# The second stage of two more token blocks by seven products of quarters

## The chip, the cores and the metric

The kernel runs on one core of a Trainium2 chip. Its engines are TensorE (PE), VectorE (DVE), ScalarE (ACT) and GpSimd (POOL); loads and stores are issued mostly by SyncE (SP). The metric is the device time of one execution in microseconds. Before the change three runs took 969.06, 969.94 and 973.84 us (median 969.94).

## The reference

Three layers in a row, on 3072 tokens, in float32:

```
# 1. attention with a decaying state, 4 batches x 8 heads x 768 steps, width 64
state = gamma * state + k_t v_t^T ;  y_t = scale * q_t state
# 2. first stage: x is [3072, 512]
xn  = x / sqrt(mean(x*x) + 1e-6) * rms_g
x2  = (silu(xn @ w_gate) * (xn @ w_val)) @ w_out      # 512 -> 1536 -> 512
# 3. second stage
h   = x2 @ w_in                                       # 512 -> 1024
s   = h * softmax(h)
out = ((s - mean) / sqrt(var + 1e-6) * g_ln) @ w_out2 # 1024 -> 512
```

The weights come as 64-bit numbers and are converted on the chip.

## The kernel before

The tokens are cut into six blocks of 512. A number is kept as a high part in a reduced format and a low part, the remainder (`split`: ACT casts, DVE or POOL subtracts), and each product is three matmuls (`mm3`): high x high, high x low, low x high. Tokens run along the free dimension in the first stage (`bc_block`: twelve tiles of gate and value into the banks GB and VB, each followed by its part of w_out into the four banks X) and along the partitions in the second, in four slices of 128 tokens.

The second stage is written twice. `de_block` takes a slice through eight products with w_in (`d_mm`), the maximum, exponential and mean (`soft`), eight transposes with a new split (`t_tr`), and the last matmul (`e_mm`). `de_quarters` cuts x2 and w_in into quarters and gets the four quarters of h from seven products of sums of quarters instead of eight; the sums of x2 (S1 to S4) are made at its start by DVE and ACT out of the X banks, the sums of w_in (T1, T2, T3 in the scratch tensors `t2scr`, T4 in place) once, by `w2_sums`. T2 and T3 lie in the tiles xnh and xnl, which between second stages hold the normalised tokens. Blocks 4 and 5 also do gate and value by seven products (`SEVEN`), for which `sums_steps` makes sums of the gate and value tiles (the table `SUMS` says in which block).

Block 0's second stage can't follow its first one, since w_in is converted only in block 1 (`w2_fin`). So its X banks are stored (`x2_store`), and `de_block` runs for block 0 behind block 1's. `FIRST7 = 2` is the first block whose second stage uses quarters.

The attention of block n+1 runs beside block n: `att_pieces` gives scores (`att_scores`) and output (`att_out`) of four chunks, which are put at numbered slots. In blocks 2 to 4 they lie in the first stage; in block 1 they begin at slot 35, the second stage. The same slots hold the norm's steps (`rms_steps`), weight loads and sums. What is emitted there gets its place on the engines from a scheduler; each engine then runs its instructions strictly in that order. In the order listings L122 is an attention matmul, and a name such as `X_68` is the bank X0.

Of the kernel before, what the change touches and what calls it, by code (L numbers as in the profile page):

```python
# [9 lines left out]
F32 = mybir.dt.float32  # L10
# [9 lines left out]
NB = 6  # L20
# [16 lines left out]
SUMS = {1: [(3, 0), (3, 1)], 2: [(0, 0), (1, 0), (4, 0)], 3: [(0, 1), (1, 1), (2, 0), (2, 1), (4, 1)]}  # L37
LATE_SUMS = {(3, 2): (5, 0), (3, 24): (5, 1)}
W2_SUMS_AT = (12, 18)
FIRST7 = 2  # L40
# [3 lines left out]
def retention_moe_kernel(ctx: ExitStack, tc: tile.TileContext, qk0, q2, kt, kv, wpk, w2i, w2o,  # L44
# [564 lines left out]
    def sums_steps(j, part, n):  # L609

        X, H = [], []
        tags = {(1, 0): ("A", "r2"), (3, 1): ("x2", "r2")}.get((n, part) if n == 1 or j < 2 else None, ("x2", "x2"))

        def pair(t):
            tag = tags[t is H]
            if tag == "x2":
                x = wt("x2", [P, 2, 512], F32, 4)
                t.extend((x[:, 0, :], x[:, 1, :], x))
            else:
                t.extend(wt(tag, [P, 512], F32, {"A": 2, "r2": 8}[tag]) for _ in range(2))  # L620
# [49 lines left out]
    def w2_sums(k):  # L670
# [3 lines left out]
        def whole():  # L674
            for r in (k, k + 2):
                W.append(wt("x2", [P, 2, 512], F32, 4))
# [16 lines left out]
        def parts2():  # L693
            for i in range(2):
                o.append(wt("st", [P, 512], F32R, 3))
# [101 lines left out]
    def w2_fin(key):  # L797
# [19 lines left out]
    def w_plan():  # L817
# [11 lines left out]
        w2 = [("in", i) for i in range(8)] + [("out", i) for i in range(8)]  # L829
# [357 lines left out]
    x2h, x2l = {}, {}  # L1187

    def d_mm(n, t, s):
        H = HB[t]  # L1190
        ts_ = slice(t * P, t * P + P)
        order = [(k, hf) for k in range(NK) for hf in range(2)] if t == 0 else \
            [(k, hf) for hf in range(2) for k in range(NK)]
        for i, (k, hf) in enumerate(order):
            cs = slice(hf * 512, hf * 512 + 512)
            mm3(H[hf], x2h[k][:, ts_], x2l[k][:, ts_], w2["h"][:, k, cs], w2["l"][:, k, cs],
                k == 0, k == NK - 1)
            if i == 3:
                slot(n, s)
        soft(n, t, H, halves(f4()), f4(), t == NCB - 1)  # L1200
        slot(n, s + 1)
# [53 lines left out]
    def e_mm(n, t, s, bank=None, final=False, nxt=None):  # L1255
# [29 lines left out]
        later = nxt in range(FIRST7, NB) and nxt not in SEVEN  # L1285
# [5 lines left out]

    def x2_split(srcs):
        for d in range(NK):
            if d % 2 == 0:
                th, tl = wt("x2", [P, 2, 512], F32R, 4), wt("x2", [P, 2, 512], F32R, 4)
            x2h[d], x2l[d] = th[:, d % 2, :], tl[:, d % 2, :]
            split(x2h[d], x2l[d], srcs[d])
# [8 lines left out]

    def x2_load():
# [414 lines left out]
```

## Time and profile before

| | |
|---|---|
| median of three runs | 969.94 us |
| the profiled execution | 974.37 us |
| its span, first to last instruction | 972.5 us |
| PE, DVE, ACT, POOL busy | 98%, 58%, 43%, 48% of the span |
| granted clock of PE, mean | 0.99 |

Times in views are microseconds from the start of the span. Block 1's second stage begins at 264, block 0's ends at 358 to 365, block 2's begins at 480. A busy PE is modelled: matmuls overlap, so their pace is read from starts, not from durations. What an engine waited for is put down to whatever signalled it last.

### The profile page before, as it was taken

The page shows a single profiled execution, that of the slowest core. Times are in us where ns is not written, and L with a number is a line of the kernel's source. Part 1 is how long each engine was busy: PE and PEld are TensorE (multiplying, and loading weights), DVE is VectorE, ACT ScalarE, POOL GpSimd, SP SyncE. Part 2 cuts the span into 40 slices and gives each one's busy share as a digit, 9 for nine tenths or more (in the row PEclk, how much of TensorE's full clock was granted, in tenths as well). Part 3 has the DMA queues.
Part 4 walks back from the last instruction along what each step waited for, and adds up shares of the span by engine and source line. Part 5 has one row for each costly group of instructions (what it writes and reads, how often), then busy time and mean ns, then how long its engine had stood idle before and what let it go on. Part 6 is the DMA issues. An engine that isn't in the chain of part 4 may idle for free.

```text
span 972.5 us, 18176 instructions
## 1 busy us (share of the span) xinstructions
PE 954.6 (98%) x6852; PEld 804.2 (83%) x6852; DVE 564.0 (58%) x1126; ACT 417.8 (43%) x831; POOL 465.9 (48%) x497
## 2 busy tenths in 40 slices
PE   8899999999999999999999999999999999999998
PEld 7777887888887888878888888888999888999986
DVE  4787776476375653476574644575655567343473
ACT  3767655476234352223454232356221356221344
POOL 6886764697044483774538455637111176000022
PEclk8899999999999999999999999999999999999999
DMA  9699999998823305799824899923999936698501
GB/s 341 231 317 403 335 312 359 318 348 256 301 73 99 99 22 170 247 323 290 335 76 120 265 336 305 358 101 120 279 301 380 298 115 219 216 306 292 185 0 44
DMA packets 99207, 230.91 MB, mean 237 GB/s; under 512 B 11696, under 2 KB 38704, under 8 KB 98096
## 3 DMA queue, kind: packets, MB, share of 16 engines
q1 hardware_dynamic: 90336, 204.59, 64.2%
q10 hardware_dynamic: 8784, 25.17, 6.7%
q8 instruction: 54, 0.88, 0.4%
q14 instruction: 33, 0.27, 0.1%
HBM read 187.77 MB, written 41.94 MB: 236 GB/s over the span
## 4 chain that ended last, share of the span: by engine, by line
PE 79%; DVE 6%; DMA 5%; POOL 4%; ACT 3%; issue 1%; SPq 0%; ACTq 0%; POOLq 0%; DVEq 0%
PE X L845 9%; PE X L847 9%; PE X L846 9%; PE VB L963 5%; PE GB L845 5%; PE GB L846 5%; PE GB L847 5%; PE VB L845 4%; PE VB L846 4%; PE VB L847 4%; PE GB L963 4%; PE SB L122 3%; PE X L1377 3%; PE GB L1377 2%; PE VB L1377 2%; PE YB L963 2%
## 5 line engine op out<-in xcount | busy, mean ns | idle before, releaser
L846 PE MATMUL X<-r,wo 128*128 128x512 f32 x252 | 98.9, 392 | 0.0
L847 PE MATMUL X<-r,wo 128*128 128x512 f32 x252 | 98.1, 390 | 0.0
L845 PE MATMUL X<-r,wo 128*128 128x512 f32 x252 | 95.5, 395 | 1.0 <-ACT r L101 1.0
L746 POOL TENSOR_TENSOR st<-st,x 128x512 int32<-128x512 int32 x52 | 70.5, 1356 | 53.8 <-DVE st L745 20.0
L101 ACT CAST r<-f 128x512 fp32r<-128x512 f32 x60 | 37.2, 620 | 90.9 <-DVE f L866 71.1
L866 DVE TENSOR_TENSOR f<-VB,f 128x512 f32<-128x512 f32 x48 | 33.0, 688 | 65.6 <-PE VB L847 50.3
L845 PE MATMUL GB<-xnh,w 128*128 128x512 f32 (+1 forms) x172 | 67.8, 394 | 1.0 <-ACT xnh L404 1.0
L845 PE MATMUL VB<-xnh,w 128*128 128x512 f32 (+1 forms) x172 | 67.6, 393 | 1.1 <-DVE f L866 1.1
L282 POOL TENSOR_TENSOR U<-U,u 128x256 f32<-128x256 f32 x27 | 17.5, 648 | 104.5 <-PE YB L122 50.6
L846 PE MATMUL GB<-xnl,w 128*128 128x512 f32 (+1 forms) x172 | 67.1, 390 | 0.3 <-DVE xnl L102 0.3
L846 PE MATMUL VB<-xnl,w 128*128 128x512 f32 (+1 forms) x172 | 66.9, 389 | 0.0
L847 PE MATMUL VB<-xnh,w 128*128 128x512 f32 (+1 forms) x172 | 66.8, 389 | 0.0
L847 PE MATMUL GB<-xnh,w 128*128 128x512 f32 (+1 forms) x172 | 66.7, 388 | 0.0
L102 DVE TENSOR_TENSOR r<-f,r 128x512 fp32r<-128x512 f32 x60 | 55.7, 930 | 18.9 <-ACT r L101 18.2
L897 ACT ACTIVATE f<-GB 128x512 f32<-128x512 f32 x48 | 28.5, 594 | 79.4 <-PE GB L847 79.3
L102 POOL TENSOR_TENSOR r<-st,r 128x512 fp32r<-128x512 f32 x4 | 5.2, 1298 | 112.7 <-ACT r L101 112.7
L845 PE MATMUL X<-w2oh,r 128*128 128x512 f32 (+1 forms) x144 | 56.6, 393 | 0.6 <-ACT r L1240 0.6
L847 PE MATMUL X<-w2oh,r 128*128 128x512 f32 (+1 forms) x144 | 56.0, 389 | 0.2 <-DVE r L1241 0.2
L845 PEld LDWEIGHTS X<-r,wo 128*128 128x128 f32 x252 | 47.0, 188 | 10.8 <-ACT r L101 1.1
L846 PE MATMUL X<-w2ol,r 128*128 128x512 f32 (+1 forms) x144 | 55.5, 386 | 0.0
L847 PEld LDWEIGHTS X<-r,wo 128*128 128x128 f32 x252 | 47.3, 188 | 9.9
L846 PEld LDWEIGHTS X<-r,wo 128*128 128x128 f32 x252 | 47.3, 188 | 9.8 <-DVE r L102 0.4
(517 smaller groups left out, 2764.7 us busy)
## 6 DMA issues: line engine op xcount, KB each, us to landing
w<-scr SPq DMA_DIRECT2D x73, 512.0 KB, 5.8
wo<-scr SPq DMA_DIRECT2D x57, 512.0 KB, 6.0
x<-in_wpk SPq DMA_DIRECT2D x36, 512.0 KB, 6.5
rv<-in_kv SPq DMA_DIRECT2D x40, 256.0 KB, 6.5
sscr<-x SPq DMA_DIRECT2D x20, 512.0 KB, 6.4
scr<-CV ACTq DMA_DIRECT2D x18, 512.0 KB, 6.5
w<-scr SPq DMA_DIRECT2D x34, 256.0 KB, 5.9
scr<-w ACTq DMA_DIRECT2D x12, 512.0 KB, 5.9
```

Source lines behind the costliest of these rows:

```text
L101: h = nc.scalar.copy(hi, src)
L102: (lo_eng or nc.vector).tensor_tensor(out=lo, in0=src, in1=hi.bitcast(F32), op=ALU.subtract)
L122: return lambda: nc.tensor.matmul(out, lhsT=lhsT, rhs=rhs, start=start, stop=stop)
L282: nc.gpsimd.tensor_tensor(out=new, in0=old, in1=u64.unsqueeze(2).to_broadcast([P, 4, 64]), op=ALU.mult)
L746: nc.gpsimd.tensor_tensor(out=ti, in0=ti, in1=lo, op=ALU.add)
L845: nc.tensor.matmul(ps, lhsT=lh, rhs=rh, start=start, stop=False)
L846: nc.tensor.matmul(ps, lhsT=lh, rhs=rl, start=False, stop=False)
L847: return nc.tensor.matmul(ps, lhsT=ll, rhs=rh, start=False, stop=stop)
L866: recent["dve"] = nc.vector.tensor_tensor(out=a, in0=GV[1], in1=silu[:, 0, :], op=ALU.mult)
L897: recent["act"] = nc.scalar.activation(s[:, 0, :], GV[0], AF.Silu)
L963: recent["seven"] = nc.tensor.matmul(ps, lhsT=x, rhs=y[:, k, :], start=start and k + i == 0, stop=k == 1 and i == 2, skip_group_check=True)
L1377: last["mm"] = nc.tensor.matmul(bank, lhsT=x[:, k, ts_], rhs=y[:, k, :], start=start and k + i == 0, stop=k == 1 and i == 2, skip_group_ch ...
```

## The change

Blocks 1 and 0 use `de_quarters` too, and `de_block`, `d_mm` and `x2_split` go. Block 0's stored input is loaded into two of the four weight tiles (`saved`), and `de_quarters` reads it from there instead of from the X banks. `w2_sums` moves from block 2 to block 1, works in other tiles, and is ordered behind a new order of w_in's conversion; every second remainder of w_in and w_out2 is subtracted by DVE instead of POOL. The sums of gate and value tiles 6 and 7 move from block 1 to block 2. Block 2's attention is put at slots 36 to 56 of block 1, its norm at 57 to 77, and its first weights are loaded at 62 to 71.

```diff
-SUMS = {1: [(3, 0), (3, 1)], 2: [(0, 0), (1, 0), (4, 0)], 3: ...}
+SUMS = {2: [(0, 0), (1, 0), (3, 0), (3, 1), (4, 0)], 3: ...}
-W2_SUMS_AT = (12, 18)
-FIRST7 = 2
+W2_SUMS_AT = (11, 20)
+FIRST7 = 1
...
-                W.append(wt("x2", [P, 2, 512], F32, 4))
+                W.append(f4())
...
-                o.append(wt("st", [P, 512], F32R, 3))
+                o.append(r2())
...
-            split(w2["h"][:, k, cs], w2["l"][:, k, cs], t, nc.gpsimd)
+            split(w2["h"][:, k, cs], w2["l"][:, k, cs], t, nc.gpsimd if i % 2 else nc.vector)
...
-            split(w2["oh"][:, i, :], w2["ol"][:, i, :], t, nc.gpsimd)
+            split(w2["oh"][:, i, :], w2["ol"][:, i, :], t, nc.gpsimd if i % 2 else nc.vector)
...
-        w2 = [("in", i) for i in range(8)] + [("out", i) for i in range(8)]
+        w2 = [("in", i) for i in (0, 1, 4, 5, 2, 3, 6, 7)] + [("out", i) for i in range(8)]
...
+    def x2_room():
+        for h in range(2):
+            t = wt("w4", [P, 2, 512], F32, 4)
+            saved.extend(t[:, k, :] for k in range(2))
+
     def x2_load():
         for d in range(NK):
-            t = st()
-            nc.sync.dma_start(t, x2scr[d])
-            srcs.append(t)
-        return srcs
+            nc.sync.dma_start(saved[d], x2scr[d])
...
-    def de_quarters(n, base):
+    def de_quarters(n, base, XS=XB):
...
+        behind = ExitStack()
+        if XS is not XB:
+            for key in ("thi", "lo"):
+                behind.enter_context(tc.issue_after(recent[key].ins))
...
             elif n == 1:
-                begin, span, r = 35, 21, (57, 58, 59, 59, 60, 60, 60, 61, 62, 63, 64)
+                begin, span, r = 36, 20, (57, 59, 60, 61, 61, 62, 62, 76, 76, 77, 77)
+                for s, f in ((31, x2_room), (34, lambda: t_load(0, 1)), (46, x2_load)):
+                    extra.setdefault((1, s), []).append(f)
+                for s, i, part in ((62, 0, 0), (62, 0, 1), (70, 1, 0), (71, 1, 1)):
+                    extra.setdefault((1, s), []).append(lambda g=2 * NM + i, part=part: w_load(g, part))
...
-            if n == 2:
+            if n == 1:
                 for k in range(2):
                     for i, f in enumerate(w2_sums(k)):
...
-        if n >= FIRST7:
-            de_quarters(n, 35)
-            continue
-        de_block(n, XB, 35)
+        de_quarters(n, 35)
         if n == 1:
-            de_block(0, x2_load(), 52)
+            de_quarters(0, 58, saved)
```

On DVE, before, in block 1's second stage, behind the second slice's exponentials (sm_2662 are that slice's maxima and sums, f_339 its solu values):

```order
L1220 SCALAR_TENSOR_TENSOR f_339_2661,sm_2662<-X_68,f_338_2660 128x512
L1220 SCALAR_TENSOR_TENSOR f_339_2661,sm_2662<-X_69,f_338_2660 128x512
L1246 TENSOR_SCALAR sm_2662<-sm_2662 128x1
L1241 TENSOR_TENSOR r_344_2687<-VB,r_343_2686 128x512
L1222 TENSOR_TENSOR sm_2662<-sm_2662 128x1
L1247 RECIPROCAL sm_2662<-sm_2662 128x1
L1212 TENSOR_REDUCE sm_2724<-X_70 128x1
L1223 TENSOR_SCALAR sm_2662<-sm_2662 128x1
L1225 TENSOR_SCALAR f_339_2661<-f_339_2661,sm_2662 128x512
```

The same place now, from the first multiplication by the exponentials to the subtraction (sm_2833 and f_342 are the second slice to be normalised, U_80 the attention's state, ssq its square sums):

```order
L1205 SCALAR_TENSOR_TENSOR f_342_2541,sm_2833<-f_342_2541,st_2831 128x512
L279 TENSOR_TENSOR U_80<-U_80,SB 64x2x64
L279 TENSOR_TENSOR U_80<-U_80,YB 64x2x64 x2
...
L1205 SCALAR_TENSOR_TENSOR f_342_2541,sm_2833<-f_342_2541,st_2832 128x512
L1231 TENSOR_SCALAR sm_2833<-sm_2833 128x1
L1377 TENSOR_TENSOR f_345_2585<-X_70,f_345_2585 128x512
L1207 TENSOR_TENSOR sm_2833<-sm_2833 128x1
L1232 RECIPROCAL sm_2833<-sm_2833 128x1
L1226 TENSOR_TENSOR r_368_2892<-X_68,r_367_2891 128x512
L1208 TENSOR_SCALAR sm_2833<-sm_2833 128x1
L350 TENSOR_REDUCE ssq<-sq_2795 128x128
L1210 TENSOR_SCALAR f_342_2541<-f_342_2541,sm_2833 128x512
```

Between the first multiplication and the subtraction there stood one remainder and one maximum of the next slice; now there stand the attention's state updates, an addition of a partial product, one remainder and a square sum.

On PE, before, in block 1's second stage, at the transposes behind an attention chunk's scores (L122 is that chunk's state, L845 to L847 are the last matmul of a slice):

```order
L122 MATMUL SB<-rv_1547,kd_2531 64x64
L122 MATMUL YB<-rv_1547,kd_2531 64x64
L1237 MATMUL X_68<-ident,f_339_2661 128x128 x4
L1237 MATMUL X_69<-ident,f_339_2661 128x128 x4
L845 MATMUL GB<-w2oh,r_341_2678 128x512
```

The same place now:

```order
L122 MATMUL SB<-rv_2648,kd_2711 64x64
L122 MATMUL YB<-rv_2648,kd_2711 64x64
L1222 MATMUL X_68<-ident,f_342_2541 128x128 x4
L847 MATMUL GB<-w2oh,r_368_2892 128x512
L845 MATMUL GB<-w2oh,r_367_2891 128x512
L846 MATMUL GB<-w2ol,r_367_2891 128x512
```

The last matmul of the slice before has begun ahead of the scores, and the first four transposes stand inside it.

## Rows read from the trace of the kernel before

**Rows 1.** The page: busy time, share of the span and instructions of each engine.

```profile
PE 954.6 (98%) x6852; PEld 804.2 (83%) x6852; DVE 564.0 (58%) x1126; ACT 417.8 (43%) x831; POOL 465.9 (48%) x497
```

**Rows 2.** What PE waited for, whole span: us in total, times, longest.

```profile
PE YB L122 <- DMA KV<-in_kv: 2.2, 1, 2.2
...
PE VB L845 <- DVE f L866: 1.1, 1, 1.1
...
PE VB L1237 <- DVE f L1225: 0.9, 1, 0.9
...
PE GB L1377 <- DMA xnh<-t2scr: 0.4, 1, 0.4
```

**Rows 3.** The chain of waits in block 2's second stage: start, us, what.

```profile
493.80 2.72 PE X L1377 x12
```

**Rows 4.** Stretch, its us; busy PE, PEld, DVE, ACT, POOL; clock, DMA share, GB/s.

```profile
264.00:306.00 42.00, 41.86 (x473) 34.03 (x472) 30.61 (x81) 18.67 (x44) 18.07 (x28) 1.00 0.31 90
306.00:358.00 52.00, 51.12 (x417) 42.21 (x418) 29.66 (x80) 21.68 (x48) 27.20 (x33) 1.00 0.24 72
478.00:520.00 42.00, 42.00 (x201) 34.80 (x200) 30.01 (x75) 24.42 (x51) 19.32 (x23) 1.00 0.33 125
```

**Rows 5.** The chain of waits in block 2's first stage.

```profile
415.36 1.05 DVE ssq L350
```

**Rows 6.** DVE by line, 261 to 358 us: busy, mean ns, idle before.

```profile
L350 DVE TENSOR_REDUCE ssq<-sq 128x128 f32<-128x512 f32 x4 | 4.4, 1094 | 3.1 <-ACT sq L347 3.1
L279 DVE TENSOR_TENSOR U<-U,YB 64x128 f32<-64x128 f32 x14 | 4.0, 287 | 0.2
...
L300 DVE TENSOR_TENSOR A<-SB,mtab_t 128x256 f32<-128x256 f32 x4 | 1.7, 419 | 4.0 <-PE SB L122 4.0
```

**Rows 7.** PE in order of time, block 2's second stage: start, us, what.

```profile
497.72 1.03 PE L1237 MATMUL X<-ident,f 128*128 128x128 f32 x8
498.51 0.48 PE L1377 MATMUL X<-w2ih,r 128*128 128x512 f32 x1
```

**Rows 8.** PE's busy time on L122 alone: one chunk's scores, its output.

```profile
264.00:265.10 1.10, 0.93 (x48) 0.79 (x48) 1.00 0.14 56
273.20:274.70 1.50, 1.35 (x80) 1.26 (x80) 1.00 0.00 0
```

**Rows 9.** DVE in order of time, block 2's second stage.

```profile
482.23 0.75 DVE L1344 TENSOR_TENSOR st<-X,st 128x256 f32<-128x256 f32 x2
...
491.11 0.69 DVE L1212 TENSOR_REDUCE sm<-GB 128x1 f32<-128x512 f32 x1 [0.63 <-PE GB L1377]
...
497.39 0.68 DVE L1391 TENSOR_TENSOR f<-X,f 128x512 f32<-128x512 f32 x1
497.98 0.14 DVE L1213 TENSOR_REDUCE sm<-sm 128x1 f32<-128x2 f32 x1
...
501.56 0.51 DVE L1225 TENSOR_SCALAR f<-f,sm 128x512 f32<-128x512 f32 x1
...
505.01 0.15 DVE L1213 TENSOR_REDUCE sm<-sm 128x1 f32<-128x2 f32 x1
...
508.49 0.51 DVE L1225 TENSOR_SCALAR x<-x,sm 128x512 f32<-128x512 f32 x1
```

**Rows 10.** ACT in order of time, block 2's second stage: the copy and a cast.

```profile
485.66 0.59 ACT L1387 COPY f<-GB 128x512 f32<-128x512 f32 x1 [0.36 <-PE GB L1377]
486.32 0.62 ACT L1361 CAST r<-st 128x512 fp32r<-128x512 f32 x1
```

**Rows 11.** ACT by line: the attention's square.

```profile
L347 ACT ACTIVATE sq<-YB 128x256 f32<-128x256 f32 x4 | 1.6, 397 | 0.0
```

**Rows 12.** DVE lines: duration min/median/max in ns, first and last start.

```profile
L102 DVE TENSOR_TENSOR w2il<-x,w2ih x2: 675/1581/2487, 418.8 to 441.9; 128x512 fp32r<-128x512 f32 x2
L866 DVE TENSOR_TENSOR f<-VB,f x48: 672/692/693, 46.4 to 627.6; 128x512 f32<-128x512 f32 x48
```

**Rows 13.** What POOL waited for, whole span.

```profile
POOL kd L245 <- DMA rv<-in_kv: 36.6, 9, 11.0
```

More of the change, by code (lines that the diff above doesn't have):

```diff
@@ L611, in sums_steps @@
         X, H = [], []
-        tags = {(1, 0): ("A", "r2"), (3, 1): ("x2", "r2")}.get((n, part) if n == 1 or j < 2 else None, ("x2", "x2"))
+        tags = ("x2", "r2") if part and (n, j) in ((2, 3), (3, 0), (3, 1)) else ("x2", "x2")
         def pair(t):
@@ L619, in pair @@
             else:
-                t.extend(wt(tag, [P, 512], F32, {"A": 2, "r2": 8}[tag]) for _ in range(2))
+                t.extend(wt(tag, [P, 512], F32, 8) for _ in range(2))
         def add(i, w):
@@ L1186, in retention_moe_kernel @@
     lnst = {}
[L1187 to L1201, printed above, removed]
     def halves(t):
@@ L1283, in give @@
             nc.scalar.dma_start(out[r0:r0 + P, :], o)
-        later = nxt in range(FIRST7, NB) and nxt not in SEVEN
+        later = nxt in range(2, NB) and nxt not in SEVEN
         if later:
@@ L1290, in e_mm @@
         slot(n, s + 1)
[L1292 to L1297, printed above, removed]
     x2scr = [dp.tile([P, 512], F32, tag=f"x2scr{d}", name=f"x2scr{d}") for d in range(NK)]
@@ L1335, in de_quarters @@
         for k in range(2):
-            split(a11[:, 0, k, :], a11[:, 1, k, :], XB[k][:, lo])
-            S.copy(s1[:, k, :], XB[k][:, hi])
+            split(a11[:, 0, k, :], a11[:, 1, k, :], XS[k][:, lo])
+            S.copy(s1[:, k, :], XS[k][:, hi])
         for k in range(2):
-            V.tensor_tensor(out=s3[:, k, :], in0=XB[k][:, lo], in1=s1[:, k, :], op=ALU.subtract)
+            V.tensor_tensor(out=s3[:, k, :], in0=XS[k][:, lo], in1=s1[:, k, :], op=ALU.subtract)
         for k in range(2):
-            split(xh[:, k, :], xl[:, k, :], XB[2 + k])
+            split(xh[:, k, :], xl[:, k, :], XS[2 + k])
         for k in range(2):
-            i = V.tensor_tensor(out=s2[:, k, :], in0=XB[2 + k][:, hi], in1=s3[:, k, :], op=ALU.subtract)
+            i = V.tensor_tensor(out=s2[:, k, :], in0=XS[2 + k][:, hi], in1=s3[:, k, :], op=ALU.subtract)
         S2 = two(r2()), two(r2())
@@ L1349, in de_quarters @@
             for k in range(2):
-                V.tensor_tensor(out=s1[:, k, :], in0=XB[2 + k][:, hi], in1=s1[:, k, :], op=ALU.add)
+                V.tensor_tensor(out=s1[:, k, :], in0=XS[2 + k][:, hi], in1=s1[:, k, :], op=ALU.add)
         S3 = two(r2()), two(r2())
@@ L1358, in de_quarters @@
         for k in range(2):
-            V.tensor_tensor(out=s4[:, k, :], in0=XB[2 + k][:, lo], in1=s2[:, k, :], op=ALU.subtract)
+            V.tensor_tensor(out=s4[:, k, :], in0=XS[2 + k][:, lo], in1=s2[:, k, :], op=ALU.subtract)
         S4 = two(r2()), two(r2())
@@ L1362, in de_quarters @@
         recent["s4"] = nc.gpsimd.tensor_tensor(out=S4[1], in0=s4, in1=S4[0].bitcast(F32), op=ALU.subtract)
+        behind.close()
         slot(n, base)
@@ L1462, in de_quarters @@
         e_mm(n, 3, base + 19, X3)
-        e_mm(n, 1, base + 21, X2, True, n + 1)
-    def de_block(n, srcs, base):
-        x2_split(srcs)
-        slot(n, base)
-        d_mm(n, 0, base + 1)
-        d_mm(n, 1, base + 3)
-        t_tr(0)
-        d_mm(n, 2, base + 5)
-        t_tr(1)
-        e_mm(n, 0, base + 7)
-        d_mm(n, 3, base + 9)
-        t_tr(2)
-        e_mm(n, 1, base + 11)
-        t_tr(3)
-        e_mm(n, 2, base + 13)
-        e_mm(n, 3, base + 15, nxt=2 - n)
+        e_mm(n, 1, base + 21, X2, True, {0: 2, 1: None}.get(n, n + 1))
     mtab_t = cp.tile([P, 8, P], F32, tag="mtab", name="mtab_t")
```

4 lines of the change are left out of this document (2 added, 2 removed).

## The prediction

> **What bounds the kernel now.** I read the page first: TensorE (PE) is busy for 954.6 us, 98% of the span [rows 1]. Then the table of what PE waited for: the longest wait, 2.2 us, is for the first loads, and in the stretches that the change touches the two longest are 1.1 and 0.9 us, both for VectorE (DVE) [rows 2]. So nearly every microsecond is a matmul being issued, and a change pays by taking matmuls away, unless it makes PE wait where it does not wait now. The pace comes from the chain of waits: twelve 512-column products in 2.72 us, 0.227 us each [rows 3]. The table by stretch shows what is left of the other engines [rows 4]: while blocks 1 and 0 run their second stage (264 to 358 us) DVE is busy for 60 of 94 us, and in block 2's second stage, already done by seven products, 30 of 42 us. Hence two questions: how many matmuls go, and whether DVE keeps up where more is put on it.
>
> **What is removed.** A second-stage product of one block took 4 slices x 8 x 3 = 96 matmuls; by seven quarter products it takes 7 x 2 x 2 x 3 = 84. Two blocks: 24 matmuls, 24 x 0.227 = 5.4 us, all of it on PE and so on the path. With the old order of block 1's stage goes its 0.9 us wait of a transpose for a subtraction [rows 2]. The 1.1 us wait is in block 2's first stage: the product of gate and value (L866) came late, and the chain in front of it runs over the square sum of an attention chunk on DVE [rows 5], which stands there among the additions for w2's sums. The w2 sums leave block 2, and two smaller sums come for them, so I take the whole 1.1 us. Together -7.4 us.
>
> **What is added in block 1's second stage.** The attention of block 2, four chunks, was spread over both second stages (94 us); now all of it lies in block 1's, since it ends by slot 56 and block 0's begins at 58. Its DVE work is four square sums (4.4 us), 28 state updates at 0.287 (8.0) and eight masks at 0.419 (3.4), 15.8 us [rows 6]. The seven-product stage needs some 30 us of DVE without any [rows 4]. PE's own work there is 84 x 0.227 = 19.0 for the products, 96 x 0.227 = 21.8 for the last matmuls, four pairs of transposes at 0.79 (3.2, first transpose to next product [rows 7]) and four chunks of 0.93 + 1.35 (9.1 us) [rows 8]: 53 us. 46 of 53 us on DVE, in program order, with waits for ScalarE (ACT) in between, is too tight to take as free. So I count the places where PE could run ahead of DVE, in us from the stage's first product. DVE operations of 512 columns follow each other every 0.60 us, of 256 every 0.33 (two last 0.75; one of 512 outlasts its pace by 0.09, which leaves 0.66 for two) [rows 9].
>
> First place: the third partial product into GB (p7) needs ACT to have copied the second. ACT has before it the cast of s4, for which DVE must do ten splits (done at 3.6), two masks and four updates (1.9), two casts' remainders and one addition (1.9) and s4 itself (0.7), so 7.9 to 8.1; then a cast 0.62, an attention copy and a square at 0.40 each and the copy 0.59 [rows 10, 11]: 9.9. PE gets there after 30 products (6.8) and two attention pieces (2.3), at 9.1. **Wait 0.8.**
>
> Second place: PE now has the transposes of the second slice to be normalised (t_tr(0)) right behind the third chunk's scores, with only two matmuls of the last product done before them. PE is there, the first wait counted, after another 56 matmuls (12.7) and 4.0 of attention and transposes, at 26.6. DVE: the maximum over GB starts when that product ends (15.0), the slice's joint maximum is done 6.4 later (491.11 to 498.13, less one addition that now comes later), 21.4. From there to the subtraction's end block 2's stage took 3.9 [498.13 to 502.07, rows 9]. Now four updates (1.2), one square sum (1.1) and that addition (0.6) stand in between: 28.2. **Wait 1.6.**
>
> Third place: PE goes on with 22 matmuls (5.0), the other four transposes (0.4) and the attention output (1.35): 35.4. DVE after 28.2: a remainder, an addition, two maxima, two masks, four updates and the joint maximum, 4.5, so 32.7; the subtraction is 3.3 behind a joint maximum (505.01 to 508.99, less a remainder that now fits into the wait for the exponentials): 36.0. **Wait 0.6.** The next four transposes write the bank that DVE empties only after two more maxima, a joint maximum and the remainder: 38.0, while PE is there at 36.4. **Wait 1.6.** After that DVE is ahead. Sum 4.6 us, round 4.7 with the semaphores.
>
> Bounds of this term: nothing, if DVE and ACT find in their idle gaps what I put in series (block 2's stage has such gaps, one of 0.63 us before 491.11); above, see the second rival. POOL's own subtraction stands behind the next chunk's kd and qd, which wait for a load that is issued only after the attention output; I take it as ready by 31, PE asks at 33.6.
>
> **What is added elsewhere.** Block 1's first stage gets w2's sums and eight remainders of w2 that POOL did; POOL loses the sums of tiles 6 and 7. PE has 24 matmuls (5.4 us) between the two uses of a gate or value bank, which cover a late DVE. Bounds: 0, or twice the 1.1 us that the same sums cost in block 2, 2.2; DVE operations there can be held up ([rows 12]: 0.675 us for one remainder, 2.487 for the other). I take 0.5, near the lower end, because no attention runs beside them. Block 0's second stage reads its input from SBUF and has no attention: like block 2's, which ran without a wait, 0. Its quarter tables (2 MB) are loaded into xnh and xnl as in the other blocks; the worst of these loads cost PE 0.4 [rows 2], and the first scores lie in front of it here: 0, at most 0.4 more. Block 0's input is loaded in block 1's first stage instead of inside the second, and block 2's first weights at slots 62 to 71 behind it; they have 13 us of block 0's stage: 0. The stores of the sums move with the sums.
>
> **Sum.** -5.4 - 0.9 - 1.1 + 4.7 + 0.5 = -2.2 us. The profiled execution took 974.37 us (span 972.5): 972.2. The median of the runs shown is 969.94, so **967.7 us**.
>
> **Rivals.** *PE does not wait in block 1's stage.* For it: block 2's stage shows PE busy 42.00 of 42, and in the kernel before, with half the attention in it, block 1's stage had one wait of 0.9. Against it: the third place above has DVE without a gap for ten microseconds. Then -7.4: 962.5.
>
> *DVE and POOL block each other; the change is slower.* Of two remainders of w2 with both inputs in SBUF one took 0.675 and one 2.487 us, 1.581 in the mean, while the product of value bank and gate, which reads PSUM and SBUF, took 0.672 to 0.693 in all 48 cases [rows 12]. On this POOL works beside DVE for more of block 1's stage than before: attention's preparation is squeezed in too. Thirteen DVE operations there work on SBUF alone (two remainders, six multiplications by the exponentials, five subtractions); at 0.9 more each (1.581 less 0.69), all in the chain that PE waits for, 11.7 us: -2.2 + 11.7 = +9.5, 979.4. It decides as soon as such losses pass 2.2 us. Against it: in block 2's stage the multiplications took 0.69 with POOL at 19 of 42 us. The Trainium skill (SBUF — State Buffer, Who interferes with whom) says that a DVE instruction with two SBUF inputs and a GpSimd instruction that reads SBUF exclude each other for the whole instruction. By that rule the blocked ones pay the rest of a POOL instruction, and the sum would be nearer to this rival's; by the rows of block 2's stage it stays at the forecast's. The trace agrees in block 2's first stage (2.487 us) and hardly shows it in the second.
>
> *POOL's load comes late.* Nine times POOL waited for an attention load before kd, at most 11.0 us [rows 13]. With 11.0 behind the output at 20.8, kd, qd and the subtraction (3.7) end at 35.5, 1.9 after PE asks, and once more for the next chunk: -2.2 + 3.8 = +1.6, 971.5. Against: by then PE waits for DVE anyhow, so part of it is shared.
>
> **How the numbers follow.** Forecast's mechanism 0.48 (its own range 965.3 to 970.5: the waits of block 1's stage from 2.3 to 7.5), no waits 0.25, late load or the first stage's 2.2 in full 0.17, blocking 0.10. A measurement of this kernel tells about 0.5% (4.8 us) from no change. Faster by more: most of the second case and the forecast's edge, 0.26. Slower by more: most of the last, 0.08. Within: 0.66. Range 963 to 973: it takes in nearly all of the case without waits and leaves out the blocking case.
>
> **What would show it.** Right: 24 matmuls fewer; no PE wait on L866 near 416; in block 1's second stage PE waits of 1 to 2 us in front of transposes, released by DVE's subtraction or remainder, and DVE over 80% busy between them; block 0's stage without waits. Wrong: that stage within 1 us of 53 (first rival), DVE multiplications or subtractions there well above 0.7 and 0.5 us beside POOL (second), transposes released by POOL behind kd (third), or new PE waits on L866 in block 1's first stage.

## The result and the profile after

In 20 runs each the changed kernel took 978.85 us (median) and the kernel before 972.62 us: ratio 1.0067, 95% interval 1.0051 to 1.0083. It is slower by about 6.5 us, where 2.2 us less had been forecast and the range ended at 973. The profiled execution took 983.61 us (span 981.7), the longest of the 20. Times by stage in the two profiled executions, from the starts of the first product of each (xnh with a gate tile, w2ih with x):

| stretch | before | after | change | forecast |
|---|---|---|---|---|
| first stages of blocks 0 and 1 | 228.20 | 237.26 | +9.1 | +0.5 |
| second stages of blocks 1 and 0 | 93.34 | 92.90 | -0.4 | -1.6 |
| first stage of block 2 | 121.70 | 120.84 | -0.9 | -1.1 |
| second stage of block 2 | 32.17 | 33.07 | +0.9 | 0 |
| behind it, to the last matmul's start | 456.42 | 457.16 | +0.7 | 0 |

So the loss is made ahead of the second stages, and its waits lie in block 1's first stage. (The first row varies: in six executions with the same code in it, told of below, it was 232.0 to 237.3.) What PE waited for (us in total, times, longest), after:

```profile
PE X L846 <- DVE r L102: 2.2, 1, 2.2
PE GB L845 <- ACT f L897: 2.2, 1, 2.2
PE X L1222 <- DVE f L1210: 1.9, 1, 1.9
...
PE GB L1363 <- ACT f L1373: 1.6, 1, 1.6
...
PE SB L358 <- DVE ssq L215: 1.0, 1, 1.0
...
PE GB L1363 <- DMA xnh<-t2scr: 0.7, 1, 0.7
```

Against [rows 2] the two old waits of 0.9 and 1.1 us are gone, as forecast. The first two are new and lie in block 1's first stage, the next two shown in its second stage; the last one, 0.4 before [rows 2], is in block 2's second stage. The table by stretch, with the columns of [rows 4], after:

```profile
153.00:165.00 12.00, 11.32 (x42) 9.26 (x43) 8.06 (x11) 6.04 (x10) 6.74 (x5) 0.73 1.04 372
...
228.00:237.00 9.00, 4.81 (x20) 3.29 (x18) 7.15 (x5) 5.25 (x10) 8.92 (x6) 1.00 0.98 377
237.00:242.00 5.00, 4.84 (x14) 3.83 (x15) 4.97 (x6) 2.44 (x6) 5.00 (x5) 0.66 0.13 52
...
274.20:314.20 40.00, 36.47 (x511) 28.73 (x510) 35.38 (x91) 18.27 (x42) 16.80 (x22) 0.96 0.43 133
314.20:367.20 53.00, 53.00 (x355) 43.77 (x354) 38.79 (x95) 31.10 (x70) 28.41 (x39) 1.00 0.33 104
```

The same view of the kernel before, in the stretch that has the two waits after:

```profile
228.00:237.00 9.00, 9.00 (x41) 7.48 (x40) 4.78 (x7) 4.22 (x10) 8.12 (x8) 1.00 0.71 249
```

PE did 20 matmuls in these 9 us instead of 41, and behind them the granted clock fell to the lower of its two levels: 0.66 in the mean from 237 to 242, where seven matmuls followed each other every 0.43 us instead of 0.23. The same happened once more at 153, behind two waits of 1.0 us, the first at the end of a chain from a late attention load (0.73, 2.8 us lost). That fall came in four of the six executions whose first stages have the same code, and in none of the other eleven looked at here; whether the change has a part in it is open. It is part of why this execution is the longest. The last row, the end of block 1's second stage and all of block 0's (from 334.8), has PE busy for all 53 us, as forecast for block 0; in the first 40 us of block 1's, the row above it, DVE is busy for 35.4.

How the two waits come about, after, in order of time, PE, then DVE, POOL and ACT (start, us, what, in brackets the idle time before and what ended it):

```profile
232.16 0.50 PE L846 MATMUL X<-r,wo 128*128 128x512 f32 x1 [2.18 <-DVE r L102]
...
237.16 0.51 PE L845 MATMUL GB<-xnh,w 128*128 128x512 f32 x1 [2.17 <-ACT f L897]
...
223.67 0.41 DVE L745 TENSOR_SCALAR st<-x 128x512 int32<-128x512 int32 x1
...
227.80 2.63 DVE L745 TENSOR_SCALAR st<-x 128x512 int32<-128x512 int32 x1
230.35 1.75 DVE L102 TENSOR_TENSOR r<-f,r 128x512 fp32r<-128x512 f32 x1
...
233.47 0.67 DVE L758 SCALAR_TENSOR_TENSOR st<-st,YB 128x512 f32<-128x512 f32 x1
...
227.20 2.95 POOL L677 TENSOR_TENSOR f<-w2ih,w2il 128x1024 f32<-128x1024 f32 x1
230.22 1.33 POOL L683 TENSOR_TENSOR f<-f 128x512 f32<-128x512 f32 x1
231.51 1.75 POOL L746 TENSOR_TENSOR st<-st,x 128x512 int32<-128x512 int32 x1
...
229.67 0.76 ACT L743 ACTIVATE x<-x,two 128x512 f32<-128x512 uint32 x1
234.17 0.72 ACT L809 ACTIVATE st<-st,gl_t 128x512 f32<-128x512 f32 x1 [3.75 <-DVE st L758]
...
236.51 0.59 ACT L897 ACTIVATE f<-GB 128x512 f32<-128x512 f32 x1
```

Read the first wait on DVE: the conversion's shift (L745), 0.41 us when alone, ran 2.63 us, until 0.28 us after POOL's addition for w2's sums (L677) had ended; the remainder that PE needed (r, L102) stood behind it, ran 1.75 us instead of 0.68, and ended at 232.10, 0.55 us after POOL's next instruction of the sums (L683). Together the two ran 3.3 us longer than alone, more than PE's wait. Read the second wait backwards: PE needed GB, GB's activation (L897) stood on ACT behind the scaling of a part of w_out2 (L809), this waited for DVE's L758, this for POOL's L746, and L746 stood on POOL behind two instructions of the sums (L677 adds, L683 subtracts: 4.3 us). POOL makes w2's sums by four additions of 128x1024 and eight subtractions of 128x512, called additions below. In the kernel before none of them stood there.

The Trainium skill (SBUF — State Buffer, Who interferes with whom) says that a DVE tensor_scalar can take the second port pair too, and that whoever holds it keeps it for its whole instruction. The shift's 2.63 us agree; its 16 runs in this stage took 0.95 us in the mean. They were no shorter before the change (1.08 in the mean of 15), so a held shift alone does not make PE wait. The second wait does not need that rule: it is a queue.

The two waits of the second stage, after, on ACT and DVE:

```profile
283.44 0.62 ACT L1346 CAST r<-st 128x512 fp32r<-128x512 f32 x1 [3.87 <-DVE st L1344]
284.28 0.37 ACT L344 COPY xT<-YB 128x256 f32<-128x256 f32 x1 [0.22 <-DVE U L279]
...
284.83 0.59 ACT L1373 COPY f<-GB 128x512 f32<-128x512 f32 x1
...
282.66 0.75 DVE L1344 TENSOR_TENSOR st<-X,st 128x256 f32<-128x256 f32 x2
...
303.61 1.02 DVE L350 TENSOR_REDUCE ssq<-sq 128x128 f32<-128x512 f32 x1
304.55 0.48 DVE L1210 TENSOR_SCALAR f<-f,sm 128x512 f32<-128x512 f32 x1
```

These are the prediction's first two places as it described them: the copy of GB on ACT behind s4's cast and the attention's copy (and its square), all late because of DVE, 1.6 us of wait where 0.8 was worked out; and the subtraction behind a square sum, 1.9 where 1.6 was. At both, DVE's chain was also stretched by POOL. After, DVE, then POOL:

```profile
279.69 1.31 DVE L1332 TENSOR_TENSOR r<-st,r 128x512 fp32r<-128x512 f32 x1
280.92 1.10 DVE L1339 TENSOR_TENSOR r<-st,r 128x512 fp32r<-128x512 f32 x1
...
302.03 0.94 DVE L1207 TENSOR_TENSOR sm<-sm 128x1 f32<-128x1 f32 x1
...
279.17 1.29 POOL L102 TENSOR_TENSOR r<-st,r 128x512 fp32r<-128x512 f32 x1 [26.71 <-ACT r L101]
280.79 0.69 POOL L282 TENSOR_TENSOR U<-U,u 128x256 f32<-128x256 f32 x1 [0.34 <-PE YB L122]
...
301.91 1.04 POOL L348 TENSOR_TENSOR xT<-xT,rg_t 128x512 f32<-128x512 f32 x1 [0.18 <-ACT xT L344]
```

Each of the three began beside a POOL instruction and ended 0.02 to 0.54 us after it. The two remainders stand ahead of s4 and took 1.0 us more than the same two in run no_upd below (0.68 each); the 128x1 addition stands ahead of the subtraction and took 0.8 us more than the slice before (0.15).

At the third place (2.2) the changed kernel had no wait, but behind the second one seven of its matmuls ran at low clock (1.4 us). In four runs below (lo_pool, direct, direct_p2, direct36) the clock stayed at 1.00 there; PE came to the third place that much earlier and waited 1.4 us, and their second stages were as long (92.8 to 93.0). Run direct36, the stretch, PE, DVE and POOL:

```profile
267.50:307.50 40.00, 35.41 (x514) 27.86 (x512) 35.49 (x91) 19.13 (x44) 16.94 (x22) 1.00 0.48 144
...
307.89 0.63 PE L1223 MATMUL X<-ident,x 128*128 128x128 f32 x4 [1.43 <-POOL U L282]
...
307.06 0.69 DVE L1227 TENSOR_TENSOR r<-X,r 128x512 fp32r<-128x512 f32 x1
...
307.16 0.61 POOL L282 TENSOR_TENSOR U<-U,u 128x256 f32<-128x256 f32 x1
```

The wait is put down to POOL, but DVE's remainder, which empties the bank as the prediction has it, ended within 0.02 us of POOL's instruction.

### The profile page after: what moved, and what is told of

Its sections match the earlier page's. It is cut to its first block, busy times and chain, and to the rows that moved or that the text cites. A ratio compares the mean times of both kernels' runs of the same rounds, so it can differ in the third digit from the quotient of the medians.

```text
span 981.7 us, 18206 instructions
## 1 busy us (share of the span) xinstructions
PE 956.1 (97%) x6828; PEld 804.7 (82%) x6828; DVE 586.3 (60%) x1168; ACT 429.3 (44%) x855; POOL 458.1 (47%) x491
## 4 chain that ended last, share of the span: by engine, by line
PE 74%; DVE 9%; DMA 8%; ACT 4%; issue 2%; POOL 2%; SPq 0%; ACTq 0%; DVEq 0%; POOLq 0%
PE X L845 8%; PE X L847 8%; PE X L846 8%; PE VB L963 5%; PE GB L845 4%; PE GB L847 4%; PE GB L846 4%; PE X L1363 4%; PE GB L963 4%; PE VB L845 3%; PE VB L846 3%; PE VB L847 3%; PE SB L122 3%; PE GB L1363 3%; PE VB L1363 3%
## 5 line engine op out<-in xcount | busy, mean ns | idle before, releaser
L746 POOL TENSOR_TENSOR st<-st,x 128x512 int32<-128x512 int32 x52 | 71.8, 1382 | 62.1 <-DVE st L745 20.8
L847 PE MATMUL X<-r,wo 128*128 128x512 f32 x252 | 98.9, 393 | 0.0
L845 PE MATMUL X<-r,wo 128*128 128x512 f32 x252 | 95.7, 399 | 1.9 <-ACT r L101 1.9
L101 ACT CAST r<-f 128x512 fp32r<-128x512 f32 x64 | 39.4, 619 | 92.8 <-DVE f L866 73.2
L102 POOL TENSOR_TENSOR r<-st,r 128x512 fp32r<-128x512 f32 x6 | 7.8, 1292 | 139.9 <-ACT r L101 139.9
L845 PE MATMUL GB<-xnh,w 128*128 128x512 f32 (+1 forms) x172 | 68.5, 399 | 3.1 <-ACT f L897 2.2
L845 PE MATMUL VB<-xnh,w 128*128 128x512 f32 (+1 forms) x172 | 67.7, 394 | 0.1
L847 PE MATMUL GB<-xnh,w 128*128 128x512 f32 (+1 forms) x172 | 67.3, 391 | 0.0
L847 PE MATMUL VB<-xnh,w 128*128 128x512 f32 (+1 forms) x172 | 66.8, 388 | 0.0
L102 DVE TENSOR_TENSOR r<-f,r 128x512 fp32r<-128x512 f32 x60 | 52.6, 878 | 22.0 <-ACT r L101 21.4
L897 ACT ACTIVATE f<-GB 128x512 f32<-128x512 f32 x48 | 28.5, 594 | 84.6 <-PE GB L847 71.8
L845 PEld LDWEIGHTS X<-r,wo 128*128 128x128 f32 x252 | 47.5, 190 | 12.0 <-ACT r L101 2.4
L845 PE MATMUL X<-w2oh,r 128*128 128x512 f32 (+1 forms) x144 | 56.4, 391 | 0.5 <-ACT r L1225 0.5
L847 PE MATMUL X<-w2oh,r 128*128 128x512 f32 (+1 forms) x144 | 56.0, 389 | 0.5 <-DVE r L1226 0.5
L847 PEld LDWEIGHTS X<-r,wo 128*128 128x128 f32 x252 | 47.9, 190 | 10.0
```

Source lines behind the costliest of these rows:

```text
L101: h = nc.scalar.copy(hi, src)
L102: (lo_eng or nc.vector).tensor_tensor(out=lo, in0=src, in1=hi.bitcast(F32), op=ALU.subtract)
L746: nc.gpsimd.tensor_tensor(out=ti, in0=ti, in1=lo, op=ALU.add)
L845: nc.tensor.matmul(ps, lhsT=lh, rhs=rh, start=start, stop=False)
L847: return nc.tensor.matmul(ps, lhsT=ll, rhs=rh, start=False, stop=stop)
L897: recent["act"] = nc.scalar.activation(s[:, 0, :], GV[0], AF.Silu)
```

## Experiments

Every run is compared with the kernel before on the same chip. The last two columns are the stretches of the table above (228.20 and 93.34 before).

| run | ratio to before, 95% interval | first stages 0, 1 | second stages 1, 0 |
|---|---|---|---|
| changed kernel again | 1.0072 [1.0050, 1.0093] | 237.0 | 93.1 |
| lo_pool | 1.0069 [1.0046, 1.0091] | 236.5 | 92.8 |
| no_sums | 0.9987 [0.9964, 1.0010] | 225.2 | 92.9 |
| att_spread | 1.0152 [1.0132, 1.0171] | 236.7 | 98.1 |
| halves | 1.0063 [1.0041, 1.0085] | 235.3 | 93.9 |
| direct | 1.0056 [1.0039, 1.0072] | 231.9 | 93.0 |
| after_p2 | 1.0052 [1.0034, 1.0070] | 234.3 | 93.4 |
| direct_p2 | 1.0052 [1.0031, 1.0073] | 232.0 | 92.9 |
| no_adds | 1.0018 [1.0003, 1.0034] | 227.7 | 95.0 |
| late | 1.0054 [1.0032, 1.0076] | 231.6 | 94.5 |
| fix_de | 1.0179 [1.0158, 1.0200] | 232.0 | 95.1 |
| late_de | 1.0211 [1.0179, 1.0243] | 235.2 | 96.6 |
| no_upd | 0.9986 [0.9972, 1.0000] | 234.2 | 87.7 |
| no_both | 0.9935 [0.9913, 0.9957] | 226.1 | 87.6 |
| direct36 | 1.0039 [1.0022, 1.0056] | 231.2 | 92.8 |

**The changed kernel again.** No edit.

> The changed kernel, unchanged, as the base for the other three of this call. Both theories: 1.0067 of before again, near 979. Its trace is a second look at where the loss sits. Theory A (the loss is made in block 1's first stage, where VectorE's subtractions with both inputs in SBUF are held up by GpSimd, which now has w2's sums there too): again two or more TensorE waits of 1 to 3 us in the second half of that stage, and the granted clock lower behind them; stage 6 us longer than before's. Theory B (the loss is in block 1's second stage, into which all of block 2's attention is squeezed): the first stage within 2 us of before's.

The two waits of the first stage came again, 2.2 us each, and the low clock behind them. The loss sits there.

**lo_pool.** The remainders of w_in and w_out2 on POOL, as before the change:

```diff
-split(w2["h"][:, k, cs], w2["l"][:, k, cs], t, nc.gpsimd if i % 2 else nc.vector)
+split(w2["h"][:, k, cs], w2["l"][:, k, cs], t, nc.gpsimd)
```

> All 16 remainders of w_in and w_out2 are subtracted by GpSimd again, as in the kernel before; everything else as changed. Theory A: VectorE loses 12 us of its work in block 1's first stage, all of it operations that GpSimd can hold up, but GpSimd (51 of 60 us busy there) gets about 12 us more and becomes late itself: 977 to 982, no better than the changed kernel by more than 2 us. Rival A2 (plain count of VectorE's work, and not who shares SBUF with whom): the two waits go and the time is 6 us lower, about 973. Theory B: no change from 979.

No change. The two waits became one of 5.6 us, of GB's product for ACT. Taking work off DVE and giving it to POOL does not help: A2 falls.

**no_sums.** The additions and splits left out, parts of w_in stored instead:

```diff
-return [whole, none, sums, none, parts, parts2, store, store2]
+return [none, none, none, none, none, none, store, store2]
```

> The additions for w2's sums and their splits are left out; quarters of w_in itself are stored in their place, so the sums that the seven products need are not computed. Stores, loads and TensorE's products as in the changed kernel; VectorE still subtracts every second remainder of w_in and w_out2. Theory A: GpSimd has 20 us less and VectorE 9 us less in block 1's first stage, both waits near 230 and 235 go and the clock stays up behind them: 6 us lower, about 973. Theory B: at most 1 us lower, 978.

0.80 to 0.85% under the changed kernel, some 8 us, more than expected; no wait is left in that stage. The table by stretch, run no_sums (after: the rows from 228 above):

```profile
220.00:240.00 20.00, 20.00 (x90) 16.57 (x89) 8.62 (x14) 11.36 (x19) 7.27 (x6) 1.00 0.82 296
```

So w2's sums in block 1 cost some 8 us by this run. The second stages are as long as in the changed kernel: two separate costs.

**att_spread.** Block 2's attention over both second stages:

```diff
-begin, span, r = 36, 20, (57, 59, 60, 61, 61, 62, 62, 76, 76, 77, 77)
+begin, span, r = 36, 30, (67, 69, 70, 71, 71, 72, 72, 76, 76, 77, 77)
```

> Block 2's attention is put at slots 36 to 66 instead of 36 to 56, so that it runs on into block 0's second stage, and the norm's first steps behind it at 67 to 72. Theory A: only the two waits of block 1's second stage go (1.8 and 2.0 us, and some 1.4 us of low clock behind them), if nothing new waits for the norm: 4 us lower, 975; the waits in block 1's first stage stay. Theory B: all of the loss goes, 972 or lower.

Wrong, and the wrong way: the second stages took 5 us more. PE then waited four times for DVE's remainders (4.1 and 1.8 us in all) and three times for ACT's casts (2.9), now in block 0's stage too. Squeezing the attention into block 1's stage is the better of the two.

**halves.** Each addition of 128x1024 made in two:

```diff
-nc.gpsimd.tensor_tensor(out=W[-1].rearrange("p a x -> p (a x)"), in0=w2["h"].bitcast(F32)[:, r, :],
-                        in1=w2["l"].bitcast(F32)[:, r, :], op=ALU.add)
+for a in range(2):
+    cs = slice(512 * a, 512 * a + 512)
+    nc.gpsimd.tensor_tensor(out=W[-1][:, a, :], in0=w2["h"].bitcast(F32)[:, r, cs],
+                            in1=w2["l"].bitcast(F32)[:, r, cs], op=ALU.add)
```

> The changed kernel; each of the four GpSimd additions of 128x1024 that put w_in's quarters together for w2's sums is made in two of 128x512, same work. Theory A (a VectorE operation that works on SBUF alone waits for the end of the GpSimd instruction that runs beside it; in the changed kernel one of 0.41 us ran for 2.63 us, until 0.3 us after an addition of 2.95 us ended): the longest VectorE operations of block 1's first stage fall from 2.6 to 2.9 us to about 1.8, and the two waits of 2.4 us near 230 and 235 shrink to about 1 each: 976, 3 us under the changed kernel. Rival A3 (it is GpSimd's total work, which makes the conversions late, not the length of one instruction): unchanged, 979 to 981.

Unchanged, so A falls in this form, and A3 holds: it is POOL's queue and not the length of one instruction. The longest DVE operations of the stage did fall as expected, from 2.9 to 1.8 us; but all four half additions now stood in a row, where the changed kernel has a conversion's addition between two long ones, so the order on POOL changed with the edit. Run halves, POOL and ACT in order of time (the edit moved the lines by two: L679 and L685 are the sums, L748 the conversion, L811 the scaling, L899 the activation of GB):

```profile
223.97 5.58 POOL L679 TENSOR_TENSOR f<-w2ih,w2il 128x512 f32<-128x512 f32 x4 [1.23 <-DVE r L102]
229.52 1.45 POOL L748 TENSOR_TENSOR st<-st,x 128x512 int32<-128x512 int32 x1
...
231.72 0.72 ACT L811 ACTIVATE st<-st,gl_t 128x512 f32<-128x512 f32 x1 [4.37 <-DVE st L760]
232.35 0.61 ACT L753 ACTIVATE YB<-x 128x512 f32<-128x512 f32 x1
232.91 0.57 ACT L899 ACTIVATE f<-GB 128x512 f32<-128x512 f32 x1
```

Four additions in a row, 5.6 us, then the conversion's addition; ACT stood 4.4 us and PE 5.8 for one activation. DVE was not the one that was busy: 5.1 of the 10 us from 224.

**direct, after_p2, direct_p2.** The conversion writes w_in into xT, so the additions of 128x1024 go; the attention at other slots; both:

```diff
-t = st()
+t = xT[:, 2 * (key[1] // 4) + key[1] % 2, :] if key[0] == "in" else st()
...
-extra.setdefault((n, begin + i * span // (len(pieces) - 1)), []).append(f)
+at_n = (36, 38, 42, 44, 45, 50, 51, 52, 53, 54, 55, 57)
+extra.setdefault((n, at_n[i]), []).append(f)
```

> The changed kernel, where the conversion writes w_in's parts straight into xT (free in that stage), so that the four GpSimd additions of 128x1024 (10.7 us) go; the other eight additions and all splits of w2's sums stay; w_in and w_out2 are converted in turns of four, one slot later, and the sums stand at slots 9 and 25. Theory A: the two waits of 2.4 us and the low clock behind them go: 6 to 8 us lower, 972 to 974, and block 1's first stage as long as in the run without sums (112.6 us from the stage's first matmul). Rival A4 (VectorE's splits of the sums and its remainders are the load): at most 3 us lower, 977. Rival A5 (the sums' tiles take two of three f4 buffers, so that gate's activation waits for one): as theory A in time, but then in the changed kernel's trace ACT should have waited for a tile before the late activation, while it stands behind a conversion there.

> The changed kernel; of block 2's attention the first chunk's output is put two slots later (42, behind the third partial product into GB), the second chunk's behind the first transposes (50 instead of 46), the rest at 51 to 57, the norm one slot later. First place of the prediction (ScalarE's copy of GB stands behind the attention's copy and square, which wait for VectorE's state updates): its wait of 1.8 us goes. Second place (square sum and updates ahead of the subtraction): its wait of 2.0 us goes or falls under 0.5, and the low clock behind it (1.4 us). If nothing becomes late in its place: 4 to 5 us under the changed kernel, 975. Rival (VectorE is simply full, 46 of 53 us, so a wait that goes comes back further on): 978 to 981.

> Both edits, of the run that converts into xT and of the one with block 2's attention at other slots. If the two losses are separate, their gains add: 10 to 12 us under the changed kernel, 967 to 969, and 5 us under the kernel before. If they are one (say, a clock that recovers only once), not over 8.

In direct the waits near 230 went, but one of 3.6 us stood at 178, and the first stages took as long as the shortest with the changed kernel's code (232.0): there POOL had prepared two attention chunks and the first of the sums ahead of the conversion's addition. Its time (1.0056, about 1 us under the changed kernel) is the one that A4 named, not A's; the next run tells A4 from A3. The edit of the slots missed: there are eight pieces, not twelve, so the first output stayed at slot 38 and the same two waits stood in the second stage (1.6, and 2.0 to 2.5 us). after_p2 and direct_p2 don't test the order that was meant.

**no_adds.** POOL's twelve additions out, the casts and DVE's subtractions of the sums kept, and with them the tiles that the sums take and the new order of w_in's conversion:

```diff
-return [whole, none, sums, none, parts, parts2, store, store2]
+return [whole, none, none, none, parts, parts2, store, store2]
```

> The changed kernel with the twelve additions of w2's sums on GpSimd left out (the sums that the seven products need are not computed); ScalarE's casts and VectorE's subtractions of the sums stay and work on slices of w_in instead, stores, loads and products stay. Theory A3, as it stands after the run with halved additions (GpSimd's queue: the additions stand in it ahead of the conversion's integer addition, the conversion's later steps hold ScalarE's queue, and gate's activation stands behind them there): the waits in block 1's first stage go, 7 to 8 us under the changed kernel, as in the run without sums. Rival A4 (VectorE's and ScalarE's share of the sums): at most 3 us lower.

The first stages are as short as before the change (227.7) and block 1's has no wait over 0.4 us, with DVE's and ACT's share of the sums still in it: A4 falls, and so does A5, as the sums' tiles were still taken. The second stages took 2 us more (a wait of 3.2 us before transposes), so the whole gains 5 us instead of 7 to 8.

**late.** The first half of the sums from xT, the second half behind the last conversion:

```diff
-nc.gpsimd.tensor_tensor(out=out, in0=a, in1=b, op=ALU.subtract)
+with tc.issue_after(recent["conv"].ins):
+    nc.gpsimd.tensor_tensor(out=out, in0=a, in1=b, op=ALU.subtract)
```

> The changed kernel; w_in's parts of the first half of the sums are converted straight into xT, so that two of the four GpSimd additions of 128x1024 go, and the second half's ten additions are ordered behind the last conversion's integer addition on GpSimd, where it had nothing to do for 27 us (the end of block 1's first stage). Theory A3: the waits of 2.4 us and the low clock behind them go, 5 to 7 us under the changed kernel, 973; a new wait of up to 4 us for the loads of the sums at the start of the second stage if the stores come too late. Rival (any place in that stage holds something up): 977 or more.

The waits near 230 went, one of 2.5 us stood at 178 as in direct, the second stages took 1.5 us more, and block 2's waited 1.6 for the loads of the sums. Hardly a gain in sum (1.0054). No work of the sums stood on POOL ahead of the wait at 178: the conversions, in their new place beside the attention's preparation, were enough, with GB's activation on ACT behind a cast of w_in.

**fix_de, late_de.** The order on ACT and DVE in the second stage and the attention's slots set by hand, alone and with late:

```diff
-S.copy(S4[0], s4)
+def s4_split():                       # called behind the copy of the second product in GB
+    with tc.issue_after(last["act"].ins):
+        S.copy(S4[0], s4)
...
+if gc == 2 * NCB + 1:
+    tied.enter_context(tc.issue_after(recent["sub"].ins))
```

> The changed kernel; in de_quarters ScalarE's cast of s4 and the first attention chunk's copies are queued behind the copy of the second partial product in GB, and the second chunk's state updates, copies and square sum behind the subtraction that the first transposes of the normalised slices wait for (the earlier edit of the slots had left the first output where it was, so it did not try this). First place and second place of the prediction: the waits of 1.8 and 2.0 to 2.2 us in block 1's second stage go, and the low clock behind the second: 4 us under the changed kernel, 975; the stage takes 89 to 90 us instead of 93 together with block 0's. Rival (VectorE is full there, 46 of 53 us): a wait of as much appears further on, 978 or more.

> The edits of the two kernels before this one together. If they are separate losses: 9 to 11 us under the changed kernel, 968 to 970, under the kernel before by 4 us, which is what the prediction's sum gives without its added terms (-7.4), less what is left of the first stage's cost.

Both waits went, and the second stages took 2 us more (3.6 in late_de); each run has ten other waits there and just behind, of 0.3 to 1.8 us: the rival. As s4's cast was moved in every block, blocks 2 to 5 lost some 10 us too; the totals say nothing of block 1.

**no_upd, no_both.** The attention's 28 state updates and four square sums left out, alone and together with w2's sums:

```diff
-state_add(Uc[0], 1)
+if gc // NCB != 2:
+    state_add(Uc[0], 1)
```

> The changed kernel; of block 2's attention VectorE's 28 state updates and four square sums are left out (12.4 us of its 15.8 by the prediction's rows; the state and the norm's sums of block 2 are then not right), TensorE's matmuls, ScalarE's copies and squares and GpSimd's part stay. If VectorE's share of the attention, in series with the slices' normalisation, makes the waits of block 1's second stage (first and second place of the prediction): both go (1.8 and 2.0 to 2.2 us) with the low clock behind them (1.4 us), 975, 4 to 5 us under the changed kernel; the two second stages together take 88 instead of 93 us. If it is the order on ScalarE or the seven products themselves: the waits stay within 0.5 us, 978 or more.

> Both left out: the additions and splits of w2's sums in block 1's first stage, and the 28 state updates and four square sums of block 2's attention. If these two are the whole difference between the changed kernel and the prediction's terms without added waits (-7.4 us: 24 matmuls fewer and two old waits): 966 to 968 where before is 973. If some third thing costs, no less than 970.

The table by stretch of the two second stages, the first 40 us and the rest, and DVE's two remainders of the first place, run no_upd:

```profile
270.86:310.86 40.00, 39.55 (x536) 31.98 (x535) 30.46 (x80) 22.59 (x54) 23.29 (x32) 1.00 0.53 158
310.86:358.50 47.64, 47.64 (x327) 39.29 (x326) 30.01 (x74) 26.50 (x57) 22.94 (x30) 1.00 0.30 95
...
275.08 0.68 DVE L1335 TENSOR_TENSOR r<-st,r 128x512 fp32r<-128x512 f32 x1
275.68 0.68 DVE L1342 TENSOR_TENSOR r<-st,r 128x512 fp32r<-128x512 f32 x1
```

Against the changed kernel's rows for these stages DVE has 13.7 us less, PE has one wait of 0.4 us left, the clock stays at 1.00, and the stages take 5.2 us less: DVE's share of the attention makes the second stage's waits, and not the order on ACT. With it gone the two remainders also run alone, so the run doesn't separate DVE's own work from what POOL adds by holding it. By the totals no_upd is some 8 us under the changed kernel, more than its stages show, and no_both 5 us under no_upd, less than no_sums gave for w2's sums; each interval is 1.4 to 2.2 us either way. With both out the kernel is 0.65% faster than before, 6.3 us (4.2 to 8.5), against the 7.4 of matmuls and old waits: nothing third is needed.

**direct36.** As direct, without the shift by a slot:

```diff
-W2_AT = [37 + 2 * j for j in range(16)]
+W2_AT = [36 + 2 * j for j in range(16)]
```

> The kernel that converts w_in straight into xT, without the shift by one slot, which in that kernel had left one wait of 3.7 us at 178 (GpSimd: preparation of two attention chunks, then the conversion's addition behind the first sums). If that wait came from the shift: block 1's first stage 228 to 229 us from the first gate product of block 0, as before the change, and 974, equal to the kernel before. If from the sums' additions in GpSimd's queue: the wait stays, 977 to 979.

The wait stays, 4.2 us. Run direct36, POOL and ACT:

```profile
170.26 1.22 POOL L245 TENSOR_TENSOR kd<-rv,ktab_t 128x512 f32<-128x512 f32 x1
171.45 1.74 POOL L250 TENSOR_TENSOR qd<-qd,qtab_t 128x512 f32<-128x512 f32 x1
173.15 1.47 POOL L683 TENSOR_TENSOR xT<-xT 128x512 f32<-128x512 f32 x1
174.57 1.28 POOL L102 TENSOR_TENSOR w2il<-xT,w2ih 128x512 fp32r<-128x512 f32 x1
175.81 2.54 POOL L746 TENSOR_TENSOR xT<-xT,x 128x512 int32<-128x512 int32 x2
...
177.86 0.62 ACT L101 CAST w2ih<-xT 128x512 fp32r<-128x512 f32 x1 [4.64 <-DVE xT L758]
...
180.36 0.59 ACT L898 ACTIVATE f<-GB 128x512 f32<-128x512 f32 x1
```

The same queue with other work in it: attention's preparation, one of the sums and a remainder ahead of the conversion's addition, GB's activation behind the cast that this releases. At 1.0039 it is the best of the complete versions; none beats the kernel before.

## Why the prediction was wrong, point by point

- **The 24 matmuls and the two old waits (-7.4).** Right: 6852 matmuls became 6828, both waits are gone from the table, and with both costs out no_both measures -6.3.
- **Block 1's second stage (+4.7).** Right in cause; the size was met partly by luck. The stretch came out 0.4 us under before; with -5.4 for the matmuls and -0.9 for the old wait that leaves 5.9, and no_upd gives 5.2 for the attention on DVE. All three places cost: 1.6 (0.8 worked out), 1.9 (1.6) and 1.4 (2.2), the last as a wait where the clock stayed up and as low clock in the changed kernel; 4.9 in sum where 4.6 was worked out. The errors cancel. The first place was too small by about the 1.0 us that POOL held two remainders, which the sum has at 0.60 each; the second has up to 0.8 us of the same in it, without which it would be under 1.6. PE's own work there was 54.8 us, not 53 (no_upd, from 270.86 to block 0's first product at 326.15, less the wait of 0.4), and the sum of 35.4 at the third place takes in four transposes (0.4) that it doesn't list; neither changes the account.
- **"Block 1's first stage ... I take 0.5, near the lower end, because no attention runs beside them."** The step that failed: the stage came out 3.8 to 9.1 us longer than before in the six executions, and w2's sums in it cost some 8 us by no_sums (5 by no_both against no_upd), where the upper bound was 2.2. The bound was taken from the same sums in block 2, where nothing was being converted. In block 1 they share POOL with 16 conversions, one integer addition each, and POOL was already busy for 8.1 of 9 us there before the change. The other half was missed altogether: gate's activation, which frees the bank that PE needs, stands on ACT behind the conversion's steps. The 5.4 us between two uses of a bank cover a late DVE, not an ACT that stands 3.75 us behind POOL's queue and then has four instructions (2.3 us) ahead of the activation. 0.5 should have been read from POOL's load in that stretch, and from what stands ahead of L897 on ACT.
- **Block 2's first stage (-1.1).** Right: 0.9.
- **The rival "blocking" (979.4).** Its time was met by luck: the median before rose from 969.94 (three runs) to 972.62 (twenty), and the change was +6.5 where the rival has +9.5. Its mechanism was there in part. In the second stage the multiplications by the exponentials took 0.68 to 0.69, but two remainders and a 128x1 addition were held, 1.8 us together where the rival has 11.7. In the first stage held operations account for the first of the two waits; halves, where no addition for the sums is longer than 1.8 us, shows that the queue alone makes a wait longer than both.
- **The rival "late load".** No PE wait behind kd in that stage. "No waits" fell with the first two places.
- **Block 0's second stage and its loads (0).** Right: PE busy for 53.00 of 53 us, which hold all of it.

Not settled: how the 8 us split between held operations and queue in the unedited kernel, how the second stage's waits split between DVE's work and its being held, and whether some order of POOL's work in block 1's first stage has room for the sums; three attempts (direct, late, direct36) moved the wait and got back 1 to 3 us of the measured time.

## What to carry to other kernels

Work that is moved to another stage has to be priced by the engine queues of the stage it goes to, not by what it cost where it stood: look at how busy its own engine is there, and at whose result stands behind it. Where an engine runs in order, follow the chain one step further than the engine that gets the work: additions on POOL cost PE 2.2 us by way of DVE and then ACT, where the instruction that frees the bank stood four places behind the one that waited. Look also at which instructions of a neighbour the moved work will run beside: two remainders and a 128x1 addition, held for 1.8 us in all, stood ahead of the second stage's first two waits, both longer than worked out. Here a wait in such a chain was not mended by an order set by hand, with DVE busy for 35 of 40 us in that stage; leaving the suspected work out tells cause from place much faster.

## What was not expected of the hardware

Two waits of 2.2 us, 5 us apart, were followed by low clock: from 238.3 to 241.3 seven matmuls at 0.43 us, 1.4 us more than at the clock before, so that the pair cost 5.8 us. All eight executions with waits of 2.2 us and more between 215 and 260 us show a granted clock of 0.92 to 0.96 in the mean of that stretch, the nine without show 1.00. Two waits are not needed for it: in fix_de the clock fell 0.1 us after the first one (2.2) had ended, and the second was only 0.6.

In block 1's second stage the single wait of 1.6 us was followed by no low clock, and the one in front of the transposes sometimes was: behind 1.9 us in the changed kernel and 2.0 in no_sums, but not behind 1.9 in lo_pool and direct36, 2.0 in direct_p2 and 2.1 in direct. So waits of the same length were followed by either level of the clock. And what low clock costs depends on what comes next: there the 1.4 us only took the place of PE's next wait.
